# Replanning the order of all engines in a fused linear-attention and feed-forward kernel, with four single PSUM banks for everything but attention

## The chip, the cores and the metric

The kernel runs on one core of a Trainium2 chip. The metric is device time in microseconds (us) of one execution; lower is better. The engines are TensorE (PE, with its weight loads shown apart as PEld), VectorE (DVE), ScalarE (ACT), GpSimd (POOL) and SyncE (SP), whose queue issues every DMA here. Each engine runs its instructions in the order in which they were recorded, and waits for others by semaphores.

## The reference

```python
# r, k, v, w: [4, 8, 768, 48] float32 (batch, head, time, dim); u: [8, 48]
for t in range(S):                                   # a linear attention with decay
    cur = einsum('bhd,bhe->bhde', u * k[t], v[t])
    y[t] = einsum('bhd,bhde->bhe', r[t], state + cur)
    state = w[t][..., None] * state + einsum('bhd,bhe->bhde', k[t], v[t])
x = y.transpose(0, 2, 1, 3).reshape(3072, 384)       # tokens x (heads * dim)
out = (maximum(x @ w_in, 0) ** 2) @ w_out            # w_in [384, 2048], w_out [2048, 384]
```

## The kernel before

The 3072 tokens are worked in 12 steps of 256 (three steps for each of the four batches). A step's attention is done in chunks, with the state carried from chunk to chunk and from step to step of the same batch; then the step's 256 rows of y go through both products of the feed-forward part. All work is cut into small operations, and one long string, ORDER (line 17), names them one after another. A word is `name.step.part:bank=engine`: `rl_.2.5=A` is the relu of step 2, group 5, on ACT (V is DVE, G is POOL), and `m1_.2.5:1` the matmuls that it reads, in bank 1. The loop at the end of the kernel walks the string and calls the function of each word. Each engine takes its own instructions in that order, so the string is the whole schedule: nothing is reordered later.

The operations of a step s are these.

- `ld` (L155 to L193): loads of w, r, k, v of a step, of u, and of w_in (`i`) and w_out (`o`) in four groups each, which `cast` (L181) turns to bf16 on ACT, DVE or POOL. All on SP, as are `store`, `dtr_` and `dyt_`.
- `ww_` (L240) product of two neighbouring decays, `lw_` its logarithm on ACT, `cum_` (L280) sums of it by matmul, `exp_` and `ac_` (L289, L293) exponentials on ACT, `rd_` (L301) r and k times the decays on DVE; `rw_` and `kw_` (L254, L258) products that `rd_` reads.
- `tr_` with `rkt_` (L309, L321), or `dtr_` (L325): transposes of both, on PE with a copy out of PSUM, or by DMA. `p_` (L330): products of k and r inside a chunk; `pm_` (L344): the mask on DVE.
- `ku_`, `qp_`, `q_`, `vq_` (L262 to L278): the bonus term of u; three on POOL, the sum `q_` on DVE.
- `su_` (L362): the step's addition to the state; `ts_` (L375) adds it on DVE or ACT, `sn_` (L383) decays it on POOL: the carry.
- `y_`, `yq_`, `yc_` (L399 to L424): the three parts of y into one PSUM tile: inside the chunk, bonus, and state. `ysb_` (L433) takes it to bf16.
- `yt_` with `xt_` (L438, L446), or `dyt_` (L451): the transpose of y, on PE with a copy, or by DMA.
- `m1_` (L457): the first product, 8 groups of six matmuls of 256 columns; `rl_` (L469) relu and scale; `sq_` (L477) the square, a quarter of the step at a time (`gt` times `gt` on DVE, or Square on ACT); `m2_` (L485): the second product, for each half c in four quarters of four matmuls of 384 columns; `os_` (L492) takes it out, and `store` writes it.

The words `pp_` (L357) and `yy_` (L426) stand for fixed runs on PE: both `p_` of a step, and `su_` of the next step with `y_`, `yq_`, `yc_` of this one.

PSUM has eight banks. Two pairs, att0 and att1, serve `cum_`, `p_`, `su_` and `y_`. Two banks `bk` serve `m2_` and the transposes, two banks `m1_` serve the first product. Tiles in SBUF come from rotating pools (four buffers each of the raw inputs, three of `gt`, two of most others).

Of the kernel before, what the change touches and what calls it, by code (L numbers as in the profile page):

```python
# [17 lines left out]
ld.0.w warm_.16.0 ld.1.w ld.0.k ld.0.u ld.0.r ld.1.r ww_.1=V ww_.0=V ld.1.k ld.0.v lw_.0 lw_.1 kw_.0=V  # L18
cum_.1:0 ku_.0 cum_.0:1 ld.0.i warm_.13.0 ac_.0 ac_.1 rw_.0=V exp_.0 qp_.0 ld.1.v exp_.1 rd_.0.0 rd_.0.1
tr_.0.0:0 ld.1.i warm_.1.1 rw_.1=V ld.2.w rkt_.0.0=A tr_.0.1:1 q_.0 ku_.1 rkt_.0.1=A ld.3.i rd_.1.0  # L20
p_.0.0:mm v_.0=A kw_.1=V qp_.1 warm_.2.0 rd_.1.1 su_.0:1 ld.2.k tr_.1.0:0 pm_.0.0 ts_.0.0=A tr_.1.1:1
rkt_.1.0=A p_.0.1:0 sn_.0.0 ld.2.r pm_.0.1 rkt_.1.1=A vq_.0 v_.1=A ts_.0.1=V y_.0:0 q_.1 cast.i.0=A sn_.0.1
p_.1.1:mm yq_.0 pm_.1.1 yc_.0 vq_.1 p_.1.0:1 ysb_.0=A ld.2.i warm_.3.0 pm_.1.0 ld.0.o cast.i.1=A yt_.0:0
su_.1:0 xt_.0=V y_.1:1 ts_.1.0=V ld.1.o yq_.1 ww_.2=V m1_.0.2:0 sn_.1.0 m1_.0.3:1 rl_.0.2=A yc_.1 cast.i.3=V
rl_.0.3=A m1_.0.1:0 lw_.2 ts_.1.1=V ld.2.o ysb_.1=A m1_.0.6:1 sq_.0.1=V ld.2.v cum_.2:0 rl_.0.1=V rl_.0.6=A
yt_.1:1 exp_.2 m1_.0.7:1 xt_.1=V rw_.2=V m1_.0.0:0 rl_.0.7=A kw_.2=V rl_.0.0=A rd_.2.0 m1_.1.0:1 cast.i.2=G
ac_.2 m1_.1.7:0 sq_.0.3=A rl_.1.0=V tr_.2.0:0 rd_.2.1 ku_.2 ld.3.o rl_.1.7=A m1_.1.5:1 sq_.0.0=A ld.3.w
m1_.0.5:0 rl_.1.5=V ld.3.r tr_.2.1:1 cast.o.0=V sn_.1.1 rl_.0.5=A m1_.1.4:1 rkt_.2.0=V m1_.0.4:0 rl_.1.4=A
rkt_.2.1=A rl_.0.4=V qp_.2 m1_.1.1:1 sq_.1.2=V m2_.0.0.0:0 cast.o.1=A m1_.1.2:0 ld.3.k pp_.2:10 rl_.1.2=A
m2_.0.0.1 rl_.1.1=A pm_.2.1 v_.2=G sq_.0.2=A m1_.1.3:0 cast.o.2=G ld.3.v q_.2 m1_.1.6:1 m2_.0.1.0:1 pm_.2.0  # L30
rl_.1.6=A vq_.2 m2_.0.1.1 cast.o.3=A ld.4.w rl_.1.3=V su_.2:0 m2_.0.1.2 ww_.3=G sq_.1.0=A ld.4.r m2_.0.0.2
lw_.3 m2_.0.1.3 sq_.1.1=A cum_.3:1 os_.0.1=V ld.4.k m2_.0.0.3 rw_.3=V exp_.3 m2_.1.0.0:1 ts_.2.0=V kw_.3=G
sq_.1.3=A rd_.3.0 m2_.1.0.1 ld.5.r sn_.2.0 m2_.1.0.2 ac_.3 os_.0.0=A rd_.3.1 m2_.1.0.3 v_.3=A ku_.3
store.0.1 tr_.3.0:0 os_.1.0=V yy_.2:01 ww_.4=V qp_.3 ld.4.v rkt_.3.0=V lw_.4 tr_.3.1:1 ysb_.2=A m2_.1.1.0:0
rkt_.3.1=V ld.5.k ts_.3.0=A cum_.4:1 rw_.4=V sn_.3.0 yt_.2:1 exp_.4 m2_.1.1.1 xt_.2=V ac_.4 ld.5.w m2_.1.1.2
rd_.4.0 kw_.4=G m1_.2.1:1 ts_.3.1=V dtr_.4.0 ku_.4 m1_.2.0:0 rd_.4.1 rl_.2.1=A rl_.2.0=A m1_.2.5:1 q_.3
dtr_.4.1 pp_.3:01 sn_.3.1 rl_.2.5=A m1_.2.3:0 pm_.3.1 ld.6.w vq_.3 m2_.1.1.3 rl_.2.3=A pm_.3.0 m1_.2.2:1
v_.4=A qp_.4 m1_.2.6:0 ld.7.w sq_.2.0=A rl_.2.2=V yy_.3:10 rl_.2.6=V ld.5.v sq_.2.1=A ww_.5=V kw_.5=G
os_.1.1=A m1_.2.4:1 rw_.5=V ld.7.r ysb_.3=A m1_.2.7:0 lw_.5 yt_.3:1 ts_.4.0=V rl_.2.4=A m2_.2.0.0:0 ld.6.k
xt_.3=A sn_.4.0 sq_.2.2=V m2_.2.0.1 ku_.5 cum_.5:0 store.1.1 m2_.2.1.0:1 ac_.5 q_.4 exp_.5 m1_.3.1:1  # L40
ts_.4.1=V rl_.2.7=A m2_.2.1.1 rd_.5.0 rl_.3.1=A m1_.3.7:0 ww_.6=G sq_.2.3=A rd_.5.1 m2_.2.1.2 dtr_.5.0
sn_.4.1 rl_.3.7=A m1_.3.3:1 pp_.4:10 vq_.4 store.0.0 rl_.3.3=A m1_.3.2:0 dtr_.5.1 v_.5=A pm_.4.0 m1_.3.4:1
rl_.3.2=A ww_.7=G pm_.4.1 m2_.2.1.3 ld.6.r lw_.6 rl_.3.4=A qp_.5 m1_.3.0:0 ld.7.k lw_.7 kw_.6=V m2_.2.0.2
sq_.3.1=A ld.6.v yy_.4:10 ku_.6 ld.7.v rl_.3.0=V os_.2.1=V m2_.2.0.3 ysb_.4=A ts_.5.0=V store.1.0 sq_.3.0=V
m1_.3.5:1 sn_.5.0 yt_.4:1 rl_.3.5=A m1_.3.6:0 xt_.4=V sq_.3.2=A ld.8.w pp_.5:10 qp_.6 rl_.3.6=V m1_.4.0:1
os_.2.0=A pm_.5.0 sq_.3.3=A m2_.3.1.0:1 ld.8.r pm_.5.1 m1_.4.5:0 rw_.6=G rl_.4.0=A m2_.3.0.0:0 rw_.7=G q_.5
cum_.6:1 m1_.4.3:1 exp_.6 rl_.4.5=V kw_.7=G m2_.3.1.1 ac_.6 rd_.6.0 rl_.4.3=A cum_.7:0 vq_.5 m1_.4.1:0
exp_.7 rd_.6.1 dtr_.6.0 m2_.3.0.1 ac_.7 rd_.7.0 ww_.8=G v_.6=A m1_.4.2:1 dtr_.6.1 m2_.3.0.2 rd_.7.1
rl_.4.1=A v_.7=G rl_.4.2=A m2_.3.0.3 q_.6 sq_.4.0=A ld.8.k yy_.5:10 vq_.6 sq_.4.1=A m1_.4.4:0 ts_.6.0=A
dtr_.7.0 os_.3.0=A m1_.4.6:1 sn_.6.0 ysb_.5=A m2_.3.1.2 ld.9.r rl_.4.6=V ku_.7 lw_.8 yt_.5:0 store.2.0  # L50
rl_.4.4=A ts_.6.1=V m2_.3.1.3 xt_.5=V ld.9.w pp_.6:01 ld.9.k sn_.6.1 m1_.4.7:1 pm_.6.0 m1_.5.1:0 ku_.8
os_.3.1=V ld.8.v m2_.4.1.0:0 rl_.5.1=A pm_.6.1 dtr_.7.1 m2_.4.1.1 rl_.4.7=A sq_.4.3=A m1_.5.3:0 kw_.8=V
yy_.6:01 rl_.5.3=A ld.11.k sq_.4.2=A m1_.5.0:1 ts_.7.0=V ysb_.6=A m1_.5.4:0 sn_.7.0 rl_.5.0=V dyt_.6
# [36 lines left out]
def kernel(  # L90
# [54 lines left out]
    def bf16_bank(i):  # L145
        return bk[int(i)][:].bitcast(BF16)
# [420 lines left out]
```

## Time and profile before

| what | us |
|---|---|
| median of three runs | 189.66 |
| the three runs | 188.51, 189.66, 193.23 |
| the profiled execution: span from first to last instruction | 186.7 |
| busy in it: PE, DVE, ACT, POOL | 177.0, 125.8, 125.1, 104.9 |
| mean of 6 matmuls of m1 on the chain (L464) | 0.65 |
| mean of one rl on ACT, on DVE (L473, L475) | 0.60, 0.69 |
| mean of one sq on ACT, on DVE (L481, L483) | 1.05, 0.75 |
| mean of one pm over an att pair on DVE (L354) | 1.22 |

The profile has no device time of its own execution, only the span; the three runs are 1.8 to 6.5 us above it. A row of the profile gives line, engine, operation, output and inputs, shapes, count, busy time and mean. Busy time on PE counts overlapping matmuls once. In a table by stage, each row is a stretch of the span with the busy time of PE, PEld, DVE, ACT and POOL, each followed by its count of instructions, and then the granted clock, the busy share of the DMA engines and GB/s. In the chain, each row is start, length, engine, output or the releasing instruction, line and count.

### The profile page before, as it was taken

Reading aid. Unit: us, or ns where it says so; the run is one execution under the profiler, and the core shown is the slowest. Engines: PE = TensorE matmul, PEld = TensorE weight load, DVE = VectorE, ACT = ScalarE, POOL = GpSimd, SP = SyncE. Lnnn points to the kernel's source line nnn. Section 1 sums busy time; section 2 is a strip of 40 time slices with the busy share of each in tenths; the row PEclk is TensorE's granted clock in tenths of the full one; section 3 lists DMA queues with packets and bytes.
Section 4 is the critical chain, followed back from the end, with each engine's and each line's share of the span. In section 5 each row is a group of like instructions: output and inputs, shape, how many; then the busy total and the mean of one; then the engine's idle time right before and its main releaser. Section 6 shows DMA issues by size and latency. Waiting matters only on the chain.

```text
span 186.7 us, 5422 instructions
## 1 busy us (share of the span) xinstructions
PE 177.0 (95%) x2303; PEld 125.4 (67%) x2303; DVE 125.8 (67%) x170; ACT 125.1 (67%) x205; POOL 104.9 (56%) x99
## 2 busy tenths in 40 slices
PE   7686998999999999999999999999999999999992
PEld 2344587766777777777776766777666777776761
DVE  4379979686799876983849699795946472562020
ACT  5278978889659795797687577968541656156732
POOL 7289627695897998959496981563934130000000
PEclk9999999999999999999999999999999999999999
DMA  6999999999999999979999999890539150203022
GB/s 151 269 274 341 330 280 381 340 280 264 275 234 218 257 239 236 248 148 147 279 185 260 220 270 251 240 147 32 66 63 201 30 172 0 46 0 126 4 84 84
DMA packets 78952, 35.81 MB, mean 192 GB/s; under 512 B 72144, under 2 KB 77392, under 8 KB 78928
## 3 DMA queue, kind: packets, MB, share of 16 engines
q1 hardware_dynamic: 78928, 35.46, 82.5%
q8 instruction: 18, 0.29, 0.7%
q14 instruction: 6, 0.05, 0.1%
HBM read 25.36 MB, written 4.72 MB: 161 GB/s over the span
## 4 chain that ended last, share of the span: by engine, by line
PE 80%; DVE 8%; ACT 5%; issue 3%; DMA 3%; SPq 0%; ACTq 0%
PE m L464 32%; PE bk L489 31%; PE att L394 8%; DVE rdec_buf L305 4%; PE att L341 3%; PE att L371 3%; DMA w_raw<-in_w_dram 3%; PE bk L444 1%; PE att L286 1%; PE att L287 1%; ACT att L291 1%; DVE r_raw L256 1%; ACT ac_buf L298 1%; DVE pmT L351 1%; DVE pmT L354 1%
## 5 line engine op out<-in xcount | busy, mean ns | idle before, releaser
L464 PE MATMUL m<-xT,wi_sb 128*128 128x256 bf16 x576 | 74.3, 273 | 0.5 <-ACT gt L473 0.5
L489 PE MATMUL bk<-wo_sb,gt 128*128 128x384 bf16 x384 | 71.9, 326 | 0.0
L464 PEld LDWEIGHTS <-wi_sb 128*128 128x128 bf16 x576 | 54.9, 98 | 13.9 <-issue 1.4
L473 ACT ACTIVATE gt<-m 128x512 f16<-128x512 f32 x68 | 39.7, 596 | 34.4 <-PE m L464 34.1
L489 PEld LDWEIGHTS <-gt 128*128 128x128 bf16 x384 | 36.9, 98 | 19.3
L481 ACT ACTIVATE gt<-gt 128x1024 bf16<-128x1024 f16 x36 | 37.6, 1053 | 0.9 <-DVE gt L475 0.7
L354 DVE TENSOR_TENSOR pmT<-att,mask 128x1024 bf16<-128x1024 f32 x22 | 26.3, 1218 | 5.6 <-PE att L341 5.5
L386 POOL TENSOR_TENSOR S<-t_state,ac_buf 128x384 bf16<-128x384 f32 x20 | 18.7, 935 | 19.9 <-DVE t_state L381 13.2
L475 DVE TENSOR_SCALAR gt<-m 128x512 f16<-128x512 f32 x28 | 19.2, 687 | 14.6 <-PE m L464 11.9
L264 POOL TENSOR_TENSOR ku<-k_raw,u_bc 128x768 f32<-128x768 f32 x12 | 22.5, 1878 | 9.1 <-DVE q L273 4.7
L269 POOL TENSOR_TENSOR ku<-ku,r_raw 128x768 f32<-128x768 f32 x12 | 22.9, 1910 | 1.0 <-DMA r_raw<-in_r_dram 0.8
L277 POOL TENSOR_TENSOR vq<-v_raw,q 128x768 bf16<-128x768 f32 x12 | 18.2, 1520 | 9.1 <-DVE q L273 4.8
L305 DVE TENSOR_TENSOR rdec_buf<-r_raw,att 128x768 bf16<-128x768 f32 x12 | 11.3, 952 | 3.8 <-ACT att L291 2.2
L498 DVE TENSOR_SCALAR o_sb<-bk 128x384 f32<-128x384 f32 x11 | 6.1, 551 | 11.0 <-PE bk L489 11.0
L291 ACT ACTIVATE att<-att 128x768 f32<-128x768 f32 x12 | 9.4, 795 | 3.7 <-PE att L287 3.6
L305 DVE TENSOR_TENSOR rdec_buf<-k_raw,att 128x768 bf16<-128x768 f32 x12 | 11.4, 947 | 0.5 <-ACT ac_buf L298 0.5
L506 PE MATMUL bk<-warm 128*128 128x512 bf16 x35 | 10.5, 452 | 1.2 <-DVE half_ones L212 1.2
L273 DVE TENSOR_REDUCE q<-ku 128x16 f32<-128x768 f32 x12 | 11.3, 943 | 0.0
L496 ACT ACTIVATE o_sb<-bk 128x384 f32<-128x384 f32 x13 | 6.4, 490 | 6.2 <-PE bk L489 6.2
L483 DVE TENSOR_TENSOR gt<-gt 128x1024 bf16<-128x1024 f16 x12 | 8.9, 753 | 2.0 <-ACT gt L473 2.0
L381 DVE TENSOR_TENSOR t_state<-S,att 128x384 f32<-128x384 bf16 x16 | 8.7, 546 | 1.8 <-PE att L371 1.8
L247 ACT ACTIVATE lw_buf<-ww 128x384 bf16<-128x384 f32 x12 | 6.2, 524 | 5.3 <-DVE ww L243 5.3
(72 smaller groups left out, 179.8 us busy)
## 6 DMA issues: line engine op xcount, KB each, us to landing
w_raw<-in_w_dram SPq DMA_DIRECT2D x12, 384.0 KB, 5.1
k_raw<-in_k_dram SPq DMA_DIRECT2D x12, 384.0 KB, 6.1
r_raw<-in_r_dram SPq DMA_DIRECT2D x12, 384.0 KB, 6.2
v_raw<-in_v_dram SPq DMA_DIRECT2D x12, 384.0 KB, 6.0
out_dram<-o_sb SPq DMA_DIRECT2D x24, 192.0 KB, 3.1
w_st<-in_moe_w_in_dram SPq DMA_DIRECT2D x4, 768.0 KB, 8.5
w_st<-in_moe_w_out_dram SPq DMA_DIRECT2D x4, 768.0 KB, 8.7
rkT<-rdec_buf SPq DMA_TRANSPOSE x16, 4.0
```

Of the source, the lines that this page charges most:

```text
L264: nc.gpsimd.tensor_mul(ku[:], raw["k", s][:, :, 1:3, :], u_bc[:, :, None, :].to_broadcast([C, H, 2, D]))
L269: nc.gpsimd.tensor_mul(ku[:], ku[:], raw["r", s][:, :, 0:2, :])
L277: nc.gpsimd.tensor_mul(vq[:].rearrange("p j h d -> p h j d"), raw["v", s][:], tiles.pop(("q", s))[:, :, :, None].to_broadcast([C, H, 2, D]))
L305: nc.vector.tensor_mul(rdec[:, i, :, :, 0:D], x.rearrange("p h j d -> p j h d"), cs[:, i, 0:DM].rearrange("p (h d) -> p h d", h=H)[:, None ...
L354: nc.vector.tensor_mul(pmT, ps_p[:].rearrange("p e (a x) -> p (e a) x", a=2), mk.to_broadcast([C, 4, 2 * C]))
L386: nc.gpsimd.tensor_mul(t[:], tiles.pop(("ts", s, c))[:].rearrange("p (a e d) -> p a e d", a=HP, e=2), tiles["a_c", s][:, :, c, :, None].to ...
L394: nc.tensor.matmul(ps_y[rows, c, cols], lhsT, rhs, start=fresh, stop=True, skip_group_check=True)
L464: nc.tensor.matmul(ps1[:, j, :], wi_sb[:, n // 4, kk, n % 4 * 128:(n % 4 + 1) * 128], tiles["xT", s][:, :, kk, :], start=(kk == 0), stop=( ...
L473: nc.scalar.activation(rl, m1, AF.Relu, scale=RS)
L475: nc.vector.tensor_scalar(out=rl, in0=m1, scalar1=RS, scalar2=0.0, op0=ALU.mult, op1=ALU.max)
L481: nc.scalar.activation(gt, rl, AF.Square)
L489: nc.tensor.matmul(m2, gt[:, n, c * C:(c + 1) * C], wo_sb[:, n, :], start=(n == 0), stop=(n == NT - 1))
```

## The change

ORDER is replaced as a whole. `pp_` and `yy_` are gone: `p_` of each half, `su_`, `y_`, `yq_` and `yc_` are words of their own. The two `bk` and the two `m1_` banks become four single banks `one`, and each `m1_`, `m2_`, `tr_`, `yt_` names any of them. The two att pairs stay. Pools are replaced by a list of named buffers for each kind, with the same depths; a word takes the first free one, and after a fixed count of uses it goes back. A path for moving the bonus by DMA (`mv_`, MOVED) is written but MOVED is empty, so it is never taken. The counts of PE operations, loads, stores, DMA transposes (16 `dtr_`, 6 `dyt_`) and warm-up matmuls (35) are as before. The choice of engine differs: `sq_` on DVE 23 for 12, `rl_` on DVE 30 for 28, casts on ACT, DVE, POOL 2, 3, 3 for 4, 2, 2, `ww_` on POOL 7 for 5, `v_` on POOL 5 for 3, `xt_` on ACT 3 for 1, `rkt_` on DVE 5 for 3.

```diff
-    att = [ps_att.tile([C, 2, 512], FP32, name=f"att{i}") for i in range(2)]
-    bk = [ps_att.tile([C, 512], FP32, name=f"bk{i}") for i in range(2)]
-    m1_bank = [ps_att.tile([C, 512], FP32, name=f"m1_{i}") for i in range(2)]
+    att = [ps_pool.tile([C, 2, 512], FP32, name=f"att{i}") for i in range(2)]
+    one = [ps_pool.tile([C, 512], FP32, name=f"one{i}") for i in range(4)]
...
+    def buf(kind, *key):
+        held = live.setdefault((kind,) + key, [])
+        if not held:
+            held += [free[kind].pop(0), uses_of(kind, key)]
+        held[1] -= 1
+        if not held[1]:
+            free[kind].append(live.pop((kind,) + key)[0])
+        return held[0]
...
+    def two_banks(at):
+        return [one[i][:] for i in ((2, 3) if at == "m" else (0, 1))] if at in "mn" else att[int(at)]
...
-        ps1 = tiles["m1", s, g] = m1_bank[int(slot["m1_", s, g])][:].rearrange("p (j t) -> p j t", j=2)
+        ps1 = tiles["m1", s, g] = one[int(slot["m1_", s, g])][:].rearrange("p (j t) -> p j t", j=2)
...
-        m2 = bk[int(slot["m2_", s, c])][:, 0:DM]
+        m2 = one[int(slot["m2_", s, c])][:, 0:DM]
```

The order up to the first m1, before and after:

```diff
-ld.0.w warm_.16.0 ld.1.w ld.0.k ld.0.u ld.0.r ld.1.r ww_.1=V ww_.0=V ld.1.k ld.0.v lw_.0 lw_.1 kw_.0=V
-cum_.1:0 ku_.0 cum_.0:1 ld.0.i warm_.13.0 ac_.0 ac_.1 rw_.0=V exp_.0 qp_.0 ld.1.v exp_.1 rd_.0.0 rd_.0.1
-tr_.0.0:0 ld.1.i warm_.1.1 rw_.1=V ld.2.w rkt_.0.0=A tr_.0.1:1 q_.0 ku_.1 rkt_.0.1=A ld.3.i rd_.1.0
-p_.0.0:mm v_.0=A kw_.1=V qp_.1 warm_.2.0 rd_.1.1 su_.0:1 ld.2.k tr_.1.0:0 pm_.0.0 ts_.0.0=A tr_.1.1:1
-rkt_.1.0=A p_.0.1:0 sn_.0.0 ld.2.r pm_.0.1 rkt_.1.1=A vq_.0 v_.1=A ts_.0.1=V y_.0:0 q_.1 cast.i.0=A sn_.0.1
-p_.1.1:mm yq_.0 pm_.1.1 yc_.0 vq_.1 p_.1.0:1 ysb_.0=A ld.2.i warm_.3.0 pm_.1.0 ld.0.o cast.i.1=A yt_.0:0
-su_.1:0 xt_.0=V y_.1:1 ts_.1.0=V ld.1.o yq_.1 ww_.2=V m1_.0.2:0
+ld.0.k ld.0.u warm_.16.3 ld.0.w ld.0.r ld.1.w ld.1.k ld.1.r ku_.0 ld.0.v ww_.0=V kw_.0=G lw_.0 cum_.0:1 ld.1.v rw_.0=V
+qp_.0 warm_.13.2 exp_.0 rd_.0.0 ld.1.i ww_.1=G rd_.0.1 ld.3.i q_.0 lw_.1 tr_.0.1:2 kw_.1=G cum_.1:0 rkt_.0.1=V
+warm_.3.1 ku_.1 exp_.1 ld.2.w tr_.0.0:1 rw_.1=V rd_.1.1 rkt_.0.0=A ld.0.i qp_.1 rd_.1.0 ac_.0 p_.0.0:m v_.0=A
+warm_.1.1 pm_.0.0 tr_.1.0:1 ac_.1 ld.2.i p_.0.1:1 vq_.0 su_.0:0 pm_.0.1 tr_.1.1:3 ts_.0.0=A v_.1=A sn_.0.0 rkt_.1.0=V
+y_.0:1 ld.2.k rkt_.1.1=A yq_.0 q_.1 cast.i.1=G yc_.0 ysb_.0=A p_.1.1:m ts_.0.1=V warm_.2.0 pm_.1.1 sn_.0.1 yt_.0:0
+ld.2.r su_.1:0 xt_.0=A vq_.1 p_.1.0:1 ts_.1.0=V cast.i.3=A m1_.0.3:1
```

Two later places of the new order, around step 5 and around the transposes of y in steps 7 and 8:

```diff
+m2_.2.0.1 vq_.4 ld.9.w exp_.5 ts_.4.1=V m1_.3.1:0 rd_.5.1 m1_.3.0:1 rw_.5=G ld.6.r m2_.2.0.2 sq_.2.3=A rl_.3.1=A
+v_.5=G rd_.5.0 m1_.3.6:2 ac_.5 ww_.6=G rl_.3.0=A p_.4.1:1 p_.4.0:0 rl_.3.6=A m2_.2.0.3 pm_.4.0 dtr_.5.0 dtr_.5.1
...
+m1_.4.4:0 p_.5.0:0 dtr_.6.0 rl_.4.4=A p_.5.1:1 pm_.5.0 m1_.4.5:1 rl_.4.6=A ku_.7 m2_.3.1.0:0 dtr_.6.1 pm_.5.1
+m1_.4.1:3 m2_.3.1.1 store.1.1 v_.6=G rl_.3.4=A rl_.4.1=A ld.8.w sq_.3.3=A y_.5:1 rl_.4.5=V yq_.5 q_.6 su_.6:0
...
+m1_.6.1:3 ld.11.k y_.7:1 rl_.6.1=A su_.8:0 yq_.7 qp_.9 ts_.8.0=V yc_.7 rl_.6.4=V m2_.5.1.2 ysb_.7=V m2_.5.1.3 v_.10=G
+cum_.9:0 dyt_.7 m1_.6.3:2 sn_.8.0 ac_.9 os_.5.1=V exp_.9 m1_.6.5:0 ld.11.r rw_.9=V m1_.6.7:1 ld.11.w rd_.9.1 rl_.6.5=A
+store.3.1 m1_.6.0:3 rl_.6.7=A rd_.9.0 dtr_.9.1 m2_.5.0.0:0 rl_.6.0=A q_.9 rl_.6.3=A p_.8.1:1 p_.8.0:0 dtr_.9.0
+m1_.7.2:1 pm_.8.0 ku_.11 m1_.7.1:2 rl_.7.2=A pm_.8.1 m1_.7.7:3 rl_.7.1=A m2_.5.0.1 qp_.10 sq_.6.1=V su_.9:0 y_.8:1
+ww_.11=V yq_.8 rw_.11=V yc_.8 kw_.10=G m1_.7.0:2 ysb_.8=A m2_.5.0.2 ts_.9.0=A rl_.7.7=A q_.10 dyt_.8 lw_.10 m1_.7.4:1
+sn_.9.0 rl_.7.0=V m2_.5.0.3 rl_.7.4=A rw_.10=G ld.11.v ts_.9.1=V m1_.7.3:2 sq_.6.0=V os_.5.0=A vq_.10 sq_.6.3=A
+p_.9.0:0 kw_.11=V p_.9.1:1 pm_.9.0 m1_.8.0:1 lw_.11 rl_.7.3=A sn_.9.1 m1_.7.6:0 rl_.8.0=A m1_.7.5:3 vq_.9 rl_.7.6=A
```

## The prediction

> **What bounds the kernel now.** I read the page first, then busy time by stage, then the chain of waits in order of time, then the starts of the matmuls one by one.
>
> ```profile
> PE 177.0 (95%) x2303; PEld 125.4 (67%) x2303; DVE 125.8 (67%) x170; ACT 125.1 (67%) x205; POOL 104.9 (56%) x99
> ```
>
> ```profile
> 0.00:23.40 23.40, 18.16 (x262) 9.48 (x263) 16.68 (x28) 15.10 (x27) 16.38 (x31) 1.00 1.03 273
> 60.00:105.00 45.00, 45.00 (x661) 33.04 (x659) 33.58 (x44) 35.53 (x61) 36.95 (x30) 1.00 1.09 223
> 105.00:115.00 10.00, 9.54 (x115) 7.03 (x114) 8.73 (x10) 6.98 (x12) 6.54 (x5) 1.00 1.03 245
> ```
>
> ```profile
> 6.22 1.04 DVE ww L243 x2
> 7.35 0.95 ACT lw_buf L247 x2
> 10.23 0.80 ACT att L291
> ...
> 20.59 0.39 ACT wi_sb L184
> 20.98 0.70 ACT y_sb L436
> ...
> 23.45 1.42 PE m L464 x12
> ...
> 73.82 0.34 PE bk L444 x6
> 74.16 0.65 PE m L464 x6
> 74.81 0.57 PE att L341 x32
> 75.38 0.76 PE m L464 x6
> 76.14 0.65 PE bk L489 x4
> ...
> 109.16 0.54 DVE t_state L381
> 109.70 2.06 issue
> 111.76 0.94 DVE rdec_buf L305
> ```
>
> The columns of the second fence are PE, PEld, DVE, ACT, POOL, granted clock, DMA share and GB/s. The reader is to see three things. From 60 to 105 us TensorE never stops. The chain runs through other engines before the first m1 product (23.4 us) and around 107 to 113 us, and almost nowhere else. And a group has one price wherever PE is fed: m1 0.65, m2 0.65; the first group after an att group costs 0.11 more (0.76).
>
> So I keep a ledger. PE work by the groups' steady prices: 96 m1 x 0.655 = 62.9; 96 m2 x 0.65 = 62.4; cum 12 x 0.42; tr 8 x 0.45; p 24 x 0.287; su 8 x 0.4 + 4 x 0.22; y 12 x 0.41; yq 12 x 0.42; yc 8 x 0.46 + 4 x 0.23; yt 6 x 0.34; 35 warm-up matmuls x 0.216. Sum 169.0 us. The last m2 matmul starts at 183.03 and takes 0.16, so PE loses 183.19 - 169.0 = 14.2 us; 3.5 us of evacuation and store follow (183.39, o_sb 0.49, to 186.7). The 14.2 fall so: at the first m1 (23.39 us, 14.4 of work behind it) 9.0 are lost; at y_5 (83.80, work 71.8) 12.0; at the end 14.2. Between y_5 and the end lie about 1.1 us of the 0.11 switches and about 1.1 us of the gap at 107 to 113.
>
> **The change part by part.** Same matmuls, same 35 warm-ups, same 16 + 6 DMA transposes, 8 + 6 on PE, same loads: the 169.0 stays, and the att-to-full switches go from 26 to 27 (0.1 us). Only the lost 14.2 can move. New buffers by name cost nothing: depths are the same, and no row waits for a buffer that rotation alone held.
>
> *Head.* The loads land in order of issue, 1.49 us apart (w_raw landed 4.71 and 6.20, u_bc 0.64 after k_raw). The first is now k, then u, then w of step 0: 4.71 + 0.64 + 1.49 = 6.85 instead of 4.71. Then ww 0.55 (7.5), Ln 0.52 (8.1), cum (8.6), exp with 0.2 to start (9.6), two rd (11.45), tr of k (11.95). But cum of step 1 stands before the other tr, and needs ww_1, on POOL behind ku 1.81, kw 1.0, qp 2.0: 11.5, Ln 12.1, cum 12.6, tr 13.65, rkt on ACT behind exp_1 14.9. p_0.0 starts at 14.9, against 14.70. From there the new order is shorter: pm_0.0 15.45 to 16.7, pm_0.1 to 17.9, y_0 17.95 (before 18.90). ysb_0 follows rkt_1.1 on ACT and ends 20.3; before, it stood behind the 1.47 us cast of w_in and ended 21.68. yt 20.65, su, p, xT on ACT 21.7. The cast of w_in group 1 went to POOL, after S at 18.85; its load is one place earlier (about 18.5), so it ends 20.3. First m1: 21.7, with 13.55 of work behind it, since y_1 and yq_1 now come after. Lost 8.15 against 9.0: gain 0.85.
>
> *21.7 to 80 us.* The same walk, each engine in its new order and each instruction at the median of its row, gives three stalls: m1_0.4 behind the cast of group 2 on ACT (0.2), p_3.1 behind ts_3.1 (0.2), p_4.0 behind rd_5.0, which waits for rw_5, now on POOL behind vq_4 (0.35). y_5 comes at 80.0 with 69.1 of work behind it: lost 10.9, against 12.0. Gain so far 1.1.
>
> *80 us to the end.* Switches 1.1 again. The ww_11 that stood 2.2 us in front of rd_10 (109.62) is moved, so that gap of 1.1 goes; next is what was planned close. (a) DMA transpose of y. Between the end of yc and the first m1 of its step the old order has 8.8, 8.8, 8.2 us of PE work for steps 6, 7, 8; the new one 6.3, 5.6, 3.8. The path takes 0.2 + y_sb 0.8 to 0.96 + issue to landing 2.7 to 4.8 (row L453) + 0.2 = 3.9 to 6.2. Step 8 stalls 0 to 1.0, step 7 0 to 0.6. I take 0.5 together: by then loads thin out, and the landing is nearer 2.7 to 3.9. (b) Between p and y lie 2.61 us of PE work in steps 5, 7 and 10 (before at least 3.02 past the first steps). Both pm must fit: 0.2 - 0.29 + 2 x 1.215 + 0.05 = 2.4, if DVE is free. 0.2 of margin, so any DVE instruction in the way shows: 0 to 0.5 each, I take 0.4 in all. (c) bank turns: with four single banks an m1 bank is rewritten mostly after two or more groups (1.3 us), and rl needs 0.2 + 0.6 + 0.05; nothing. The four casts, 11 sq and 2 rl that leave ACT are hidden under PE there; the tail is PE alone in both (13.7 us of m2 after the last m1), so nothing is gained there either. Lost: 10.9 + 1.1 + 1.0 = 13.0.
>
> *SP's queue.* The w of step 9 is now loaded ahead of the r of step 6, and the output tile (0,0) is stored only after step 7, so for most of the run three of four buffers of each are left to turn. The r of step 6 lands 1.5 us later (one load), near 66 us by the walk; its first product on POOL stands behind qp_5 until 68, which hides it. If it were late, POOL's rw_6 would hold ku_6 and with it vq_6 and y_6, up to the 1.5. The stores of a tile wait for an os that ended earlier in all places but the last; the last two stores stand as before, 1.8 us each from issue to landing. Bounds 0 to 1.5, taken as 0, as the cover is 2 us.
>
> *DVE and POOL.* Listed by stretches of 10 us of PE work, with the rows' means (pm 1.215, rd 0.95, q 0.94, sq 0.70, rl 0.69, others 0.55 to 1.02), DVE holds in the stretches from 20, 40, 50 and 60: before 8.8, 9.4, 7.1, 10.6; now 11.1, 10.6, 10.4, 9.0. POOL in 40 and 50: before 8.0, 8.8; now 10.5, 9.5. This is the cover of the 11 sq that move to DVE, and it is thin: over 40 to 60 DVE has 21.0 us of work in 20. The rows price more:
>
> ```profile
> 109.62 2.21 DVE L243 TENSOR_TENSOR ww<-w_raw 128x384 f32<-128x384 f32 x1
> ```
>
> ```profile
> 109.60 1.81 POOL L264 TENSOR_TENSOR ku<-k_raw,u_bc 128x768 f32<-128x768 f32 x1
> ```
>
> A 0.55 us DVE product that started inside POOL's ku ended 0.41 after it. An sq at 61.33 took 1.15 for 0.68 beside POOL's S; the mean of 12 is 0.753. So 11 more sq cost 11 x (0.753 - 0.68) = 0.8 us of DVE at the mean, 11 x 0.47 = 5.1 if each met POOL. I put nothing on the path beyond (b), as the walk kept y_2 to y_5 in time; both ends stay for the range.
>
> The Trainium skill (SBUF — State Buffer, "SBUF: two separate sides") says that DVE and GpSimd share a port pair as an exclusive lock, which a DVE instruction with two SBUF inputs takes too, and that the loser blocks for the whole instruction. The two rows agree; by that rule sq, which reads gt twice, is the wrong thing to bring to DVE while POOL is 95% booked, and the sum would go towards the 5.1 end.
>
> **Sum.** 169.0 + 13.0 + 3.5 = 185.5 us, 1.2 under the profiled span of 186.7. No run's time stands beside that execution; the runs are 1.8 (fastest) to 3.0 (median) above its span. The median less 1.2 is 188.5.
>
> **The rivals.**
>
> *Slower: DVE is the bound from 45 to 75 us and again near 100.* For it: the 11.1, 10.6, 10.4 above, and the margins of 0.2 before y. Against: the walk at medians lost only 0.75 there. It decides when DVE's waits for POOL exceed the 0.9 us of slack that pm has before each y in steps 3 to 6; with half the 5.1 on the path, 1.0 for the 21 in 20, and (a) at 1.6, the lost time is 10.9 + 1.1 + 1.0 + 2.6 + 1.0 + 1.6 = 18.2: span 190.7, time 193.7. With the sq alone at half, 15.6: 191.1.
>
> *The y transposes land late.* At the 4.8 us that two of the six took, (a) is 1.6, not 0.5: 189.6, no change. For: the same six rows. Against: the two slow ones had loads queued in front.
>
> *Faster: the gaps vanish and the head is shorter still.* If (a) and (b) are nothing and casts and loads land 1 us sooner in the head, lost is 11.0: span 183.5, time 186.5; with half of the 0.11 switches gone too, 185.5, past 2%.
>
> *PE is not the limit.* A matmul row is pipelined, so 95% may hide room. For it: PEld is 67% busy. Against: inside a group 256 columns start every 0.109 us and 384 every 0.162, everywhere alike. If weight loads were the limit, the 169.0 could shrink towards 125.4 plus warm-ups, and a replan could give 175 or less. The Trainium skill (Perfetto Trace Analysis, "Identifying the Most-Contended Engine") has this rule: matmul busy is not a good measure, weight-load busy is. The fixed spacing speaks against it here.
>
> **How the numbers follow.** Forecast 0.50 (187.3 to 189.6). DVE the bound 0.22, of which 0.12 past 193.4. Late transposes 0.12. Faster head 0.14, of which 0.11 past 2%. PE not the limit 0.02. Two per cent, about what a measurement of this kernel can tell from no change, is 185.9 to 193.4. So faster 0.13, same 0.75, slower 0.12. The range leaves out half of each outer case, 185.7 to 192.6. The likeliest is 188.5.
>
> **What would show it.** Right: PE work still 169 us by group; the first m1 near 21.7 us; y_5 near 80; no idle over 0.5 us on PE after 25 us; m1_8.0 waiting for a DMA at most 1 us. sq on DVE at 0.75 mean. Wrong: PE idle before y groups in 40 to 75 us released by DVE pmT, DVE busy over 95% there, sq or ww means over 1 us (the DVE rival); m1 of steps 7 and 8 released by the DMA on xT (late transposes); m1 before 21 us (faster); a group of six m1 matmuls under 0.6 us (PE not the limit). The forecast falls with any one wait over 2 us.

## The result, and the profile after

The changed kernel takes 197.16 us (median of 4 runs, 196.01 to 198.54) against 189.66 before (188.51 to 193.23): ratio 1.0445, 95% interval 1.0376 to 1.0515. Some executions of a kernel take longer at a lower granted TensorE clock (one below took 188.4 us at 1.00 and 193.4 at 0.98); all ratios leave those out and compare with the kernel before on the same chip, and PE's lost time is read only from profiles without such a stretch. The changed kernel is slower, and the forecast of 188.5 with a range up to 192.6 was wrong. The profiled execution took 197.7 us and has a span of 195.9.

Two rows of the page of the changed kernel, then the second of them as it was before:

```profile
PE 178.5 (91%) x2303; PEld 126.1 (64%) x2303; DVE 147.5 (75%) x182; ACT 109.8 (56%) x188; POOL 113.9 (58%) x104
...
PE 53%; DVE 32%; issue 5%; ACT 3%; DMA 3%; POOL 2%; SPq 1%; DVEq 0%; ACTq 0%; POOLq 0%
```

```profile
PE 80%; DVE 8%; ACT 5%; issue 3%; DMA 3%; SPq 0%; ACTq 0%
```

The second row is the chain that ended last. DVE now carries 32% of it, where before it carried 8%. DVE's busy time rose by 21.7 us, of which its longer list explains 9.5 at the mean lengths of before. The table by stage (PE, PEld, DVE, ACT, POOL, clock, DMA share, GB/s), first two rows of before and then the changed kernel:

```profile
23.40:45.00 21.60, 21.08 (x226) 15.84 (x225) 16.29 (x25) 18.62 (x27) 13.18 (x10) 1.00 1.11 312
...
115.00:150.00 35.00, 35.00 (x504) 25.27 (x502) 24.59 (x33) 21.10 (x36) 16.70 (x13) 1.00 0.65 120
```

```profile
23.40:45.00 21.60, 18.49 (x266) 14.36 (x267) 20.97 (x24) 15.57 (x24) 16.00 (x13) 1.00 1.05 315
...
60.00:105.00 45.00, 43.71 (x654) 32.03 (x654) 39.85 (x51) 28.16 (x49) 39.36 (x32) 1.00 0.86 204
105.00:115.00 10.00, 10.00 (x154) 7.12 (x152) 8.16 (x12) 5.64 (x10) 9.46 (x8) 1.00 1.02 213
115.00:150.00 35.00, 33.20 (x438) 24.09 (x433) 29.44 (x36) 20.82 (x37) 18.32 (x14) 1.00 0.72 149
```

From 23.4 to 45 us DVE has 20.97 of 21.6 us booked and PE idles 3.1, where it idled 0.5 before; PE idles again between 60 and 105, and between 115 and 150, where it was always busy before. Only 105 to 115, the place of the old gap, is better (10.00 of 10, before 9.54).

The ledger of the prediction (start of a word less the PE work ahead of it) shows where:

| PE loses up to | predicted | before | after | difference, after less before |
|---|---|---|---|---|
| first m1 | 8.15 | 9.0 | 10.0 | +1.0 |
| y_2 | | 11.0 | 14.5 | +3.5 |
| y_5 | 10.9 | 12.0 | 18.5 | +6.5 |
| y_8 | | 13.4 | 19.65 | +6.3 |
| end | 13.0 | 14.1 | 23.4 | +9.3 |

The spans differ by 9.2, so this is all of it. Some 70% come before y_5 (1.0 of the 6.5 at the first m1), the rest between y_8 and y_10. How it happens is seen in DVE's timeline of the changed kernel, and POOL's for the same time (start, us, engine, line, operation, tile, and in brackets the idle time before it and what ended it):

```profile
24.85 1.68 DVE L250 TENSOR_TENSOR ww_b<-w_b 128x384 f32<-128x384 f32 x1
...
31.06 1.39 DVE L266 TENSOR_TENSOR k_b<-k_b,w_b 128x384 f32<-128x384 f32 x1
32.56 0.95 DVE L315 TENSOR_TENSOR rdec_buf<-k_b,att 128x768 bf16<-128x768 f32 x1
33.43 1.75 DVE L262 TENSOR_TENSOR r_b<-r_b,w_b 128x384 f32<-128x384 f32 x1
...
38.14 3.06 DVE L473 TENSOR_TENSOR gt_b<-gt_b 128x1024 bf16<-128x1024 f16 x2
```

```profile
24.65 1.46 POOL L189 CAST wi_sb<-w_st_b 128x1536 bf16<-128x1536 f32 x1
...
30.22 1.82 POOL L274 TENSOR_TENSOR ku_b<-ku_b,r_b 128x768 f32<-128x768 f32 x1 [0.89 <-DMA r_b<-in_r_dram]
...
33.30 1.46 POOL L189 CAST wo_sb<-w_st_b 128x1536 bf16<-128x1536 f32 x1 [0.16 <-DMA w_st_b<-in_moe_w_out_dram]
...
37.76 1.48 POOL L280 TENSOR_TENSOR vq_b<-v_b,q_b 128x768 bf16<-128x768 f32 x1 [1.73 <-PE one L324]
39.20 1.46 POOL L266 TENSOR_TENSOR k_b<-k_b,w_b 128x384 f32<-128x384 f32 x1
```

Read them in pairs. ww (undisturbed 0.55) starts 0.20 us into POOL's cast; the cast ends at 26.11, ww at 26.53. kw starts inside qp, which ends at 32.04; it ends at 32.45. rw starts inside the next cast, which ends at 34.77; it ends at 35.18. The two squares (0.68 each) end 0.55 after vq and after POOL's kw. The rd between them, which reads one operand from PSUM, takes its 0.95 as ever. So a wait for POOL stands in the profile as a longer DVE instruction and not as idle time: DVE looks busy while it stands still.

The chain passes through all five of these products (start, us, what):

```profile
24.93 1.60 DVE ww_b L250
...
31.14 1.32 DVE k_b L266
...
32.56 0.95 DVE rdec_buf L315
33.51 1.68 DVE r_b L262
...
36.09 0.68 DVE gt_b L465
...
38.14 2.67 DVE gt_b L473 x2
```

And PE's row of the place, the start of tr_2 behind 54 matmuls of m1:

```profile
36.82 0.61 PE L324 MATMUL one<-ident,rdec_buf 128*128 128x128 bf16 x8 [1.84 <-DVE gt_b L465]
```

The tr writes a bank that rl has to empty first; that rl runs at 36.09, behind rw and rd on DVE. So a late product holds a bank, and all that stands behind tr on PE waits.

Every such event can be counted. Take DVE's ww, rw, kw (0.55 undisturbed), sq (0.68) and its casts of weights (0.945), and call **waiting** what one takes beyond that, if over 0.1 us. Before, 7 of 35 wait, 5.0 us in all; after, 26 of 45 wait, 19.6 us, of them 17.2 past 23 us. Every one of the 33 ends a fixed time after a POOL instruction that it met: 0.41 to 0.42 us for the decays, 0.55 for the squares, 0.81 to 0.82 for the casts. The reverse holds too: each of these instructions that starts inside one of POOL's with more than 0.23 us of it left waits. The one exception is a square that started 0.01 us after POOL's ww, and there POOL took 1.55 us for 1.00. Of the 26, 14 met the bonus (ku, qp, vq), five S, seven others.

### The profile page after: what moved, and what is told of

It reads as the page before. It is cut to its first block, busy times and chain, and to the rows that moved or that the text cites. A ratio compares the mean times of both kernels' runs of the same rounds, so it can differ in the third digit from the quotient of the medians.

```text
span 195.9 us, 5443 instructions
## 1 busy us (share of the span) xinstructions
PE 178.5 (91%) x2303; PEld 126.1 (64%) x2303; DVE 147.5 (75%) x182; ACT 109.8 (56%) x188; POOL 113.9 (58%) x104
## 4 chain that ended last, share of the span: by engine, by line
PE 53%; DVE 32%; issue 5%; ACT 3%; DMA 3%; POOL 2%; SPq 1%; DVEq 0%; ACTq 0%; POOLq 0%
PE one L479 23%; PE one L456 17%; DVE pmT_b L359 6%; DVE rdec_buf L315 6%; DVE gt_b L473 5%; PE att L393 5%; DMA w_b<-in_w_dram 3%; DVE gt_b L465 3%; DVE r_b L262 2%; DVE q_b L277 2%; DVE k_b L266 2%; PE att L348 2%; PE one L495 2%; DVE ww_b L250 2%; DVE wo_sb L189 1%
## 5 line engine op out<-in xcount | busy, mean ns | idle before, releaser
L456 PE MATMUL one<-xT_b,wi_sb 128*128 128x256 bf16 x576 | 70.9, 273 | 1.5 <-DVE gt_b L465 1.5
L479 PE MATMUL one<-wo_sb,gt_b 128*128 128x384 bf16 x384 | 70.7, 326 | 0.7 <-DVE wo_sb L189 0.7
L463 ACT ACTIVATE gt_b<-one 128x512 f16<-128x512 f32 x66 | 38.1, 596 | 29.6 <-PE one L456 28.6
L479 PEld LDWEIGHTS <-gt_b 128*128 128x128 bf16 x384 | 36.5, 98 | 21.7 <-issue 1.1
L359 DVE TENSOR_TENSOR pmT_b<-att,mask 128x1024 bf16<-128x1024 f32 x22 | 26.1, 1215 | 5.7 <-PE att L348 5.7
L465 DVE TENSOR_SCALAR gt_b<-one 128x512 f16<-128x512 f32 x30 | 20.1, 684 | 10.2 <-PE one L456 8.8
L471 ACT ACTIVATE gt_b<-gt_b 128x1024 bf16<-128x1024 f16 x25 | 26.1, 1053 | 2.8 <-DVE gt_b L465 2.5
L269 POOL TENSOR_TENSOR ku_b<-k_b,u_bc 128x768 f32<-128x768 f32 x12 | 23.3, 1941 | 6.2 <-DVE q_b L277 3.1
L473 DVE TENSOR_TENSOR gt_b<-gt_b 128x1024 bf16<-128x1024 f16 x23 | 24.0, 1051 | 2.5 <-ACT gt_b L463 2.4
L274 POOL TENSOR_TENSOR ku_b<-ku_b,r_b 128x768 f32<-128x768 f32 x12 | 23.8, 1984 | 2.1 <-DMA r_b<-in_r_dram 1.8
L277 DVE TENSOR_REDUCE q_b<-ku_b 128x16 f32<-128x768 f32 x12 | 11.3, 943 | 0.0
```

The source lines that it names most:

```text
L269: nc.gpsimd.tensor_mul(buf("ku", s)[:], buf("k", s)[:, :, 1:3, :], u_bc[:, :, None, :].to_broadcast([C, H, 2, D]))
L274: nc.gpsimd.tensor_mul(ku[:], ku[:], buf("r", s)[:, :, 0:2, :])
L359: nc.vector.tensor_mul(pmT, ps_p[:].rearrange("p e (a x) -> p (e a) x", a=2), mk.to_broadcast([C, 4, 2 * C]))
L456: nc.tensor.matmul(ps1[:, j, :], wi_sb[:, n // 4, kk, n % 4 * 128:(n % 4 + 1) * 128], xT[:, :, kk, :], start=(kk == 0), stop=(kk == KT - 1))
L463: nc.scalar.activation(rl, m1, AF.Relu, scale=RS)
L465: nc.vector.tensor_scalar(out=rl, in0=m1, scalar1=RS, scalar2=0.0, op0=ALU.mult, op1=ALU.max)
```

## The experiments

Two explanations were set against each other: that DVE's products of two SBUF operands end with POOL's instructions, and that DVE's or POOL's load, or the new buffers, are to blame by themselves. "Waiting" in what follows is that past 23 us, and "lost" is what PE loses from y_1 to the end (before 5.1, changed kernel 13.3). Both come from one profiled execution of each kernel, while ratios compare the runs with those of the kernel before on the same chip (188.6 to 188.7 us there).

**The old order on the new code.** The old words stand, with the two old pairs of banks as `one` 0, 1 and 2, 3.

```diff
-ld.0.k ld.0.u warm_.16.3 ld.0.w ld.0.r ld.1.w ld.1.k ld.1.r ku_.0 ld.0.v ww_.0=V kw_.0=G lw_.0 cum_.0:1 ld.1.v rw_.0=V
...
+ld.0.w warm_.16.0 ld.1.w ld.0.k ld.0.u ld.0.r ld.1.r ww_.1=V ww_.0=V ld.1.k ld.0.v lw_.0
...
```

> The old order, word for word, on the new code: named buffers, four single banks (the old bk are banks 0 and 1, the old m1 banks 2 and 3). It takes the order away and keeps the rest of the change. Both theories put the 7.5 us into the order, so both expect 188.5 to 191, the lost time of PE within 1 us of 14.1. If the buffers or banks cost something, it stands above 191.5.

Measured: 1.0008 (0.9968 to 1.0047). Buffers, banks and split words cost nothing that this can tell (within 0.5%). What is left is the order, with its choice of engines.

**The squares as before, in the new order.** Each sq on its engine of before (12 on DVE for 23).

```diff
-ld.3.o su_.2:1 tr_.2.0:2 cast.o.0=G ac_.2 m1_.1.5:3 sq_.1.1=V rkt_.2.0=A m1_.1.7:1 sq_.1.0=V ld.4.w sq_.0.0=A
+ld.3.o su_.2:1 tr_.2.0:2 cast.o.0=G ac_.2 m1_.1.5:3 sq_.1.1=A rkt_.2.0=A m1_.1.7:1 sq_.1.0=A ld.4.w sq_.0.0=A
...
```

> The new order with the squares on the engines that they had before (12 on DVE instead of 23, the words stay in their places). Lock theory (a DVE product of two SBUF operands stands until POOL's running instruction ends, and the new order puts more of them in POOL's way): DVE busy falls from 147.5 to 128 to 134, the time from 197.2 to 190.5 to 193.5; what remains is ww, rw, kw and casts that still meet POOL. Order theory (tight chains: the first steps, p to y, bank turns; the squares only show it): 195 or more. DVE's load without any lock: 11 squares of 0.68 less, 7.5 us of DVE; it cannot tell this from the lock, the next two runs do.

Measured: 1.0495 (1.0387 to 1.0602); no gain, as only the order theory had said. My theory in its first form, that the added squares pay the price, fell here. The squares' waiting went from 8.5 to 1.6 us in the profiled execution, but that of ww and kw grew (2.5 to 3.8, 2.3 to 2.9). In all, waiting fell from 17.2 to 11.3 us and the time did not follow, so the sum of the waiting alone does not give the time.

**POOL's bonus cut to one head of eight, in the new order.** From step 2 on, so the bonus of seven heads is left out.

```diff
-        nc.gpsimd.tensor_mul(ku[:], ku[:], buf("r", s)[:, :, 0:2, :])
+        h = H if s < 2 else 1
+        nc.gpsimd.tensor_mul(ku[:, 0:h], ku[:, 0:h], buf("r", s)[:, 0:h, 0:2, :])
...
```

> The new order; from step 2 on, the three bonus products on POOL (ku, qp, vq) are made for one head of eight, so seven eighths of the bonus term are left out; all else, DVE's list too, stays. POOL's instructions keep their places and waits but last some 0.3 us instead of 1.5 to 2.0. Lock theory: squares on DVE average 0.80 or less (1.05 in the new kernel), rw, kw and ww from step 2 on under 0.75, lost time of PE falls from 23.4 to 16 to 18 (steps 0 and 1 keep theirs), time 189.5 to 192. Order theory: no more than 2 us gained, 195 or more. DVE's load: also 195 or more, as DVE has the same list.

Measured: 1.0144 (1.0067 to 1.0221), 190.97 us; waiting 2.8, lost 6.1. Most of the loss leaves with POOL's long instructions. A new wait of PE shows up, the late transpose of y in step 8, which in the changed kernel lay behind DVE's lateness:

```profile
PE one L459 <- DMA xT_b<-y_sb_b: 1.6, 1, 1.6
```

**The same cut in the old order**, on the new code, as a control.

> The same cut (seven eighths of the bonus term left out from step 2 on) in the old order on the new code, as the control for what a lighter POOL gives by itself. Lock theory: the old order loses little to the lock, so the gain against the old order in full is 0.5 to 2 us, time 187.5 to 189.5; the two orders then stand within 3 us of each other. Order theory: the same 0.5 to 2 here, and the new order stays 5 us or more behind it.

Measured: 1.0015 (0.9956 to 1.0075). The gain of 0.5 to 2 us that was expected does not show: a light POOL alone is worth little or nothing to the old order.

**The new order's squares in the old order.** Kernel before, each sq on its engine of the changed kernel (17 go to DVE, 6 to ACT).

```diff
-rl_.1.6=A vq_.2 m2_.0.1.1 cast.o.3=A ld.4.w rl_.1.3=V su_.2:0 m2_.0.1.2 ww_.3=G sq_.1.0=A ld.4.r m2_.0.0.2
+rl_.1.6=A vq_.2 m2_.0.1.1 cast.o.3=A ld.4.w rl_.1.3=V su_.2:0 m2_.0.1.2 ww_.3=G sq_.1.0=V ld.4.r m2_.0.0.2
...
```

> The kernel before, with the 23 squares on DVE that the new order has there (17 move from ACT to DVE, 6 back), each word in its old place. Lock theory: the added squares fall where POOL runs, their mean rises from 0.75 to 0.95 or more, DVE busy from 126 to 140 or more, and the time rises by 2 to 6 us. Load theory (DVE is only fuller by 11 squares, 7.5 us of 187): squares stay near 0.75, the time rises by 0 to 1.5. Order theory: no change, 189 to 190.5.

Measured: 1.0295 (1.0250 to 1.0341); waiting 10.6, lost 10.0. In an order that was not planned for them the squares alone do cost 5.6 us. So more products on DVE cost in either order; what the run with the squares as before refutes is that the squares are the only ones that pay.

**ww_10 moved behind rd_9.1, in the kernel before.** The longest wait that the prediction showed.

```diff
-v_.9=A ww_.10=V m1_.6.0:1 vq_.8 rd_.9.1 m1_.6.4:0 rl_.6.0=A ld.10.r m2_.4.1.3 os_.5.0=V ld.11.r pp_.8:10
+v_.9=A m1_.6.0:1 vq_.8 rd_.9.1 ww_.10=V m1_.6.4:0 rl_.6.0=A ld.10.r m2_.4.1.3 os_.5.0=V ld.11.r pp_.8:10
```

> The kernel before with one word moved: ww of step 10 on DVE goes behind the rd of k of step 9 instead of ahead of it. In the trace of before that ww took 2.21 us beside a ku on POOL, and PE then stood 0.7 to 1.1 us. Lock theory for a single event: rd ends 2 us sooner, the ww still ends with POOL's instruction, the gap on PE at 107 to 113 us goes, the span falls by 0.7 to 1.2 and the time to 188.3 to 189.0. If the gap was not the ww's: no change.

Measured: 0.9955 (0.9929 to 0.9982), 187.87 us, a little below the expected 188.3 to 189.0. It is the fastest of the kernels that compute the whole reference, ahead of both that were given. The wait stays, shorter, and holds nobody up, as rd now stands ahead of it:

```profile
109.80 0.95 DVE L305 TENSOR_TENSOR rdec_buf<-k_raw,att 128x768 bf16<-128x768 f32 x1
110.67 1.32 DVE L243 TENSOR_TENSOR ww<-w_raw 128x384 f32<-128x384 f32 x1
```

**All squares on ACT, in the new order.** All 23 `=V` of sq become `=A`.

> The new order with all 48 squares on ACT, 1.05 us each whatever POOL does: ACT busy goes from 110 to some 134, DVE from 147.5 to 118 to 124. Lock theory: the loss from the squares goes wholly, time 189 to 192.5, the rest being rw, kw, ww and casts in the first 45 us; the lost time at the last m2 is 15 to 18.5. Order theory: 195 or more. A third way: ACT becomes late for m1's banks (rl stands behind squares), then PE idle released by ACT gt and 193 to 196.

Measured: 1.0428 (1.0366 to 1.0491); again no gain, where 189 to 192.5 us was expected and 197.07 came. The squares' 8.5 us of waiting are gone, but ww and kw wait 5.2 and 3.4 instead of 2.5 and 2.3; of 17.2 us 12.4 are left. And ACT is late, as the third way had it, with squares in front of m2:

```profile
PE one L479 <- ACT gt_b L471: 2.2, 2, 1.8
```

In the changed kernel PE has no wait of 0.3 us or more for ACT's squares or relus, so this run does not price the squares' meetings by themselves.

**All of DVE's products replaced, in the new order.** The decays from step 2 on and all 23 squares become reductions that last about as long (0.54 us for 0.55, 0.70 for 0.68) and read one SBUF operand, so decays and squares are not the reference's. A square's replacement reads 528 elements where the square reads 1024, and not the same number as the expectation says. POOL's code stays as it is.

```diff
-            nc.vector.tensor_mul(gt, rl, rl)
+            nc.vector.reduce_max(rl[:, :, 0], rl[:, :, 4:136], axis=AX.X)
...
+        if s > 1 and where["rw_", s] == "V":
+            nc.vector.reduce_max(r_raw[:, :, 2, 0], w_raw[:, :, 0, :], axis=AX.X)
+            return
...
```

> The new order, its code and POOL's instructions at full length; from step 2 on every product that VectorE has (squares, w, r and k decays) is replaced by a reduction of the same number of elements that reads one operand from SBUF, so the decays and squares that leave it are not the reference's; everything else stays. What is to be told apart: whether VectorE's products lose the 7.5 us by ending with GpSimd's long instructions, or whether GpSimd itself comes late in this order. Theory A (products of two SBUF operands end with GpSimd's instruction): with none left, VectorE's replacements stay at one length, without outliers, and the time comes near that of the run with short GpSimd instructions (span 189.1): 189.5 to 192.5 us. Theory B (GpSimd's own lateness: its sums and v products are due too late, and a shorter VectorE list changes nothing of that): 195 us or more. Between 192.5 and 195: both, in the share that the difference gives.

Measured: 1.0058 (1.0020 to 1.0096), 190.19 us; waiting 0.5, lost 4.2. This is the run that decides. First its DVE and POOL at the place shown above, then its stage:

```profile
30.27 0.54 DVE L276 TENSOR_REDUCE k_b<-w_b 128x8 f32<-128x384 f32 x1
30.91 0.95 DVE L327 TENSOR_TENSOR rdec_buf<-k_b,att 128x768 bf16<-128x768 f32 x1
31.78 0.55 DVE L269 TENSOR_REDUCE r_b<-w_b 128x8 f32<-128x384 f32 x1
```

```profile
28.76 1.81 POOL L286 TENSOR_TENSOR ku_b<-ku_b,r_b 128x768 f32<-128x768 f32 x1
...
31.55 1.46 POOL L189 CAST wo_sb<-w_st_b 128x1536 bf16<-128x1536 f32 x1 [0.18 <-DMA w_st_b<-in_moe_w_out_dram]
```

```profile
23.40:45.00 21.60, 21.60 (x311) 16.81 (x312) 19.60 (x27) 17.73 (x28) 15.06 (x12) 1.00 1.04 307
```

The same words meet the same POOL instructions and take 0.54 and 0.55. DVE is still booked for 19.6 of 21.6 us and PE does not stop once (in the changed kernel it had 18.49 of 21.6). So neither DVE's load nor POOL's lateness is the cause: the meeting is, and it costs both sides. POOL's busy time falls from 113.9 to 106.6 us with its code untouched; past 23 us a ku takes 1.81 to 1.85 us where it took up to 2.52.

Two limits of this run remain. The replaced rw and kw read only w and no longer wait for r and k to land; in the changed kernel they stood idle for loads for 0.2 us in all, so this is small. And the profiled execution, at 188.44 us, is the fastest of ten, so its worth is read from the ratio: the replacement gives back 7.3 of the 8.4 us that the change costs.

**The same replacement in the old order**, on the new code.

> Control of the run with VectorE's products replaced: the same replacement on the order of before (on the new buffers and banks, which alone gave 1.0008 [0.9968, 1.0047]). Theory A: the order of before has few such meetings on its path, the largest of them ww_10 with about 0.8 us, so 187 to 189.5 us. Theory B: no change, 188 to 190 us. A fall of more than 2 us would say that the replacement itself makes any order faster, and would take its size off the other run's reading.

Measured: 0.9973 (0.9933 to 1.0013); waiting 0.4, lost 4.2. The replacement by itself gives about 0.5 us in the old order, against 7.3 in the new, so it is hardly a discount on the run above. Between the two orders without products 1.6 us remain by the ratios. The two profiled executions differ by 1.2 us of lost time, of which 1.05 are lost by the first m1 already (9.76 for 8.71).

**Only the decays replaced, in the new order.** ww, rw and kw as above; the 23 squares stay products.

> The new order with only the decay products (ww, rw and kw on VectorE from step 2 on) replaced by reductions with one SBUF operand; the 23 squares stay on VectorE as products. The decays are not the reference's. Theory A in its form that any such product pays: the squares go on paying, and the run lies between that with all products replaced and the new order itself, 192 to 195.5 us. If the decays, which stand in the chain that every step of the scan begins with, are what costs, it is at 190 to 192; if the squares are, at 195.5 or more. Theory B (GpSimd late): no change, 196 to 198.

Measured: 1.0183 (1.0129 to 1.0237), 191.64 us; waiting 6.8, lost 6.8. The median lies just below the range for "any product pays alike" and inside the one for "the decays cost", but the four runs (190.22 to 192.65) lie on both sides of the border. From the changed kernel to this one 10.4 us of waiting go and 4.9 us of time by the ratios; from this one to that without any product 6.4 and 2.4. So a microsecond of waiting costs about 0.5 and 0.4; the intervals of the ratios (0.4 to 0.7% to each side) do not tell decays and squares apart in this. What the runs do tell is that taking the squares alone gave nothing, the decays alone 4.9 us, and both 7.3.

**Each ku, qp and vq as two instructions of four heads, in the new order.** The result is the reference's.

```diff
-        nc.gpsimd.tensor_mul(ku[:], ku[:], buf("r", s)[:, :, 0:2, :])
+        r_raw = buf("r", s)
+        for h in (slice(0, 4), slice(4, 8)):
+            nc.gpsimd.tensor_mul(ku[:, h], ku[:, h], r_raw[:, h, 0:2, :])
...
```

> The new order with each of GpSimd's ku, qp and vq issued as two instructions of four heads each; the result is the reference's. If VectorE's products end with the GpSimd instruction that they meet, they now wait for half of it: the 17.2 us that VectorE's products and casts spent beyond their undisturbed length after 23 us in the new order fall to 8 to 11, and the time falls by two thirds to three quarters of that, to 191 to 194 us. If GpSimd's own lateness is the cause, or if the second issue of each instruction costs GpSimd more than the shorter meetings bring (36 more instructions), it stays at 196 to 199.

Measured: 1.0170 (1.0124 to 1.0217), 192.11 us, and lost 8.8. Waiting fell to 11.9, a little less than expected; the squares before, in the changed kernel, and in this one:

```profile
L483 DVE TENSOR_TENSOR gt<-gt 128x1024 bf16<-128x1024 f16 x12 | 8.9, 753 | 2.0 <-ACT gt L473 2.0
```

```profile
L473 DVE TENSOR_TENSOR gt_b<-gt_b 128x1024 bf16<-128x1024 f16 x23 | 24.0, 1051 | 2.5 <-ACT gt_b L463 2.4
```

```profile
L479 DVE TENSOR_TENSOR gt_b<-gt_b 128x1024 bf16<-128x1024 f16 x23 | 19.8, 866 | 2.5 <-ACT gt_b L469 2.4
```

As many products wait (27 for 26), each for a shorter instruction: a square takes 866 ns on the mean for 1051. POOL does 7.3 us more (121.2 busy for 113.9), and the kernel is still 5 us faster than the changed one.

**The same halving with ww_10 moved, in the order of before.**

> The same halving on the order of before with ww_10 moved behind rd_9.1 (which gave 0.9955). Only 3.2 us are spent in waiting there, of which little stands on the path. If the meetings are what costs: 187.0 to 188.0 us. If the second issues cost GpSimd time that is on the path: 188.5 to 190.

Measured: 0.9997 (0.9966 to 1.0028), 188.58 us; missed. Waiting 3.0 for 3.2 and lost 4.4 as without the halving: where few products wait on the path, there is nothing to win. Its span is that of the run without halving (186.1), so POOL's second issues are not on the path of that execution either; of the 0.7 us between the medians 0.2 lie outside the span (the time is 2.0 us above it here, 1.8 there), and the rest I cannot explain.

## Why the prediction was wrong

**The failed step** is the last sentence of "DVE and POOL": "I put nothing on the path beyond (b), as the walk kept y_2 to y_5 in time". The walk took each DVE instruction at the median of its row of before. In the changed kernel the median square is still 0.69 us, but the mean is 1.05 and the longest 2.04; of ww, rw and kw 14 of 19 wait. A product's length is no property of its row: it is set by what POOL does at the time, and that is exactly what a new order changes. The walk had both engines' times and did not ask, product by product, which POOL instruction it would land in. In the terms of the sum PE loses 23.4 us instead of 13.0: 1.8 more at the first m1, 5.8 more from there to y_5, 2.8 more after it.

How well the rest was walked is seen where the products are taken away. There PE loses 2.5 us from the first m1 to y_5 and 4.4 to the end; the prediction had 2.75 and 4.85. This is the fastest execution of that kernel, so part of the agreement may be luck.

The other steps, one by one:

- *PE work of 169.0 us*: right. Groups keep 0.655 and 0.65; what changed is lost time alone.
- *Head, gain 0.85*: wrong, and partly for the same reason. w of step 0 landed at 7.32 us for 6.85, as u landed 1.89 after k and not 0.64; ww_0 took 1.14 us beside ku and rw_1 1.73 for 0.55 each. p_0.0 came at 15.79 instead of 14.9 and the first m1 at 23.53 instead of 21.7. No run of the new order reached its first m1 before 22.5, also those with lighter meetings past the head.
- *The gap at 107 to 113 goes*: right. y_7 to y_8 loses 0.3 for 1.0. Moving that one word in the kernel before gives 0.9955 (0.9929 to 0.9982).
- *(a) late transposes, 0.5*: not seen in the changed kernel, where the steps before were late themselves; 1.6 in step 8 of the run with the short bonus, none in that without products. The place was right; the bound of 1.0 for step 8 was too low.
- *(b) pm in front of y, 0.4*: past the head PE waited for pm in steps 6 and 10, 0.2 and 0.7 us, each time behind a square that had met POOL (2.04 and 1.52 us); in steps 5 and 7 not at all, and without products in none. In step 10 the margin of 0.2 was real, and what ate it was a product ahead of pm; step 6 has 6.0 us of PE work between p and y, but its second pm stands behind that square, a rl and two rd on DVE.
- *(c) bank turns, nothing*: the four banks themselves cost nothing (1.0008). But 1.8 and 1.5 us of PE's waits read "DVE gt L465", a bank that rl had not emptied since a product stood ahead of it on DVE.
- *SP's queue, 0*: right as far as it shows: no wait of 0.3 us or more on PE's list of the changed kernel is for a load. In its profiled execution the new order without products loses 14.15 us to the end with the new order's loads, the kernel before 14.14.
- *The sum's offset*: 3.0 us from span to median set one execution's span against other executions' time. In every run here the time is 1.7 to 2.1 us above its own span, 1.8 in the profiled one.

**The rivals.** "DVE is the bound" had the sign, a chance of 0.22, and half of the place (45 to 75 us and near 100; measured 23 to 88 and past 124). Its price was too small, 193.7 at most, because it counted the squares alone: 5.1 us if each met POOL. Measured are 8.5 for the 23 squares (0.8 for the 12 before; ten wait, 0.85 each and not 0.47), and 9.4 for ww, rw and kw (4.1 before), which no term held, although the row that I showed was a ww. "21 us of work in 20" was not needed: 19.6 in 21.6 without waits leaves PE fed. Of its signs, means of sq and ww over 1 us came (1.05 and 1.06); PE idle before y between 40 and 75 us did not. Its 18.2 us of lost time also holds (a) twice, as 0.5 inside the 1.0 and as 1.6. "PE is not the limit" is out: matmuls still start every 0.109 and 0.162 us. "Faster head" is out, as above; its 185.5 does not follow, as half of the 1.1 us of switches past y_5 leads from 186.5 to 185.95, and half of all 27 to 185.0.

The rule of the Trainium skill that the prediction weighed (SBUF — State Buffer, "SBUF: two separate sides") pointed the right way, and the runs agree with it in all that they show, the casts too: it counts DVE instructions in a two-port mode among those that take the lock, with a copy of fp32 in SBUF as its example, and DVE's casts of weights took up to 1.97 us for 0.944. Whether these casts run in that mode no run here shows. I had applied it to the squares only, because they were what the change added, and not to each product that the change moved.

What stays open: why the new order brings 26 meetings where the old has 7. More products (45 for 35) on a DVE that is fuller is part of it, and that a late product lands in the next POOL instruction is a likely other part (five products wait one after the other from 123 to 132 us), but no run separates the two. Open too is why the runs with fewer squares on DVE gain nothing although their waiting falls by 5 to 6 us; late ACT is a likely part. And under the replacement of all products the new order gives 1.0058 and the old one 0.9973: no gain of the new order shows even there.

## What to carry to other kernels

When a schedule is moved, do not walk it at the median or mean of its rows: for each DVE instruction with two SBUF operands, or a cast inside SBUF, write beside it which POOL instruction it falls into, and let it end with that one. Look for an engine whose busy time grew more than its list: a wait of this kind stands in the profile as length, not as idle time, and only the spread within a row (0.68 to 2.04) gives it away. If the meetings can't be avoided, put what feeds PE ahead of the product on its engine (ratio 0.9955 here for one word), or cut POOL's long instruction in two (1.0170 for 1.0445 here, but no gain in the order with few meetings, 0.9997 for 0.9955).

## What the runs showed of the hardware

- A DVE product of two SBUF operands that meets a running POOL instruction ends a fixed time after it, 0.13 us less than its undisturbed length: 0.41 us (undisturbed 0.55) for 384 elements of fp32, 0.55 (0.68) for 1024 of fp16, 0.82 (0.945) for the casts. Over 33 cases each of the three varies by 0.01 us.
- Beside the same POOL instructions these DVE forms never wait: the sum q (0.937 to 0.948 us), rd (0.939 to 0.955), pm (1.207 to 1.226), ts (0.537 to 0.558), rl (0.674 to 0.692), and the reductions put in for products (0.537 to 0.555, 0.699 to 0.710). All read at most one operand from SBUF.
- POOL waits likewise: ku took 2.52 us for 1.81 where a DVE cast was running, and ended 1.68 after it. Where DVE's product or cast started first (five times in the two profiles, beside the tie above), it kept its length and POOL ended 0.13 to 0.14 less than its own length after it: ku 1.68 (1.81), qp 1.67 (1.81), S 0.69 (0.83), kw 0.88 (1.01).
